# Two drains of GpSimd, behind the last gather and behind the third-last scatter

## The chip, the cores and the metric

The kernel runs on one core of a Trainium2 chip. The metric is the device time of one execution in microseconds (us), the lower the better. The engines are named as in the profile: PE is TensorE's matmuls and PEld its weight loads, DVE is VectorE, ACT is ScalarE, POOL is GpSimd, and SP is SyncE, which here only issues transfers. A "q" behind an engine's name (POOLq) marks an instruction that the engine's sequencer runs itself, such as a wait on a semaphore, a branch or a drain. A **drain** is one of these: an instruction with no operands, which each engine has at the program's start and end.

## What is computed

Linear attention without a softmax for 8 batches of 8 heads, a normalisation of each head's output, and then a mixture of experts on the resulting 4608 rows of 512: each row goes to the one expert of 8 that its logits favour.

```python
def _attn_ref(q, k, v, g_norm):
    kv = np.einsum('bhsd,bhse->bhde', k, v)
    out = np.einsum('bhsd,bhde->bhse', q, kv)
    rms = np.sqrt(np.mean(out * out, axis=-1, keepdims=True) + 1e-06)
    return (out / rms * g_norm).astype(np.float32)

def _moe_ref(x, w_gate, w_output_gate, w1, w2):       # x: 4608 x 512, 8 experts, hidden 1024
    logits = x @ w_gate
    e_idx = np.argmax(logits, axis=1)
    ...
    for e in range(E):
        mask = e_idx == e
        h = np.maximum(x[mask] @ w1[e], 0.0)
        ye = h @ w2[e]
        out[mask] = gate_w[mask, None] * eom[mask, e, None] * ye
```

## The kernel before, in words

The attention is computed tile by tile, and its rows are written to a tensor `xs` in device memory. A routing part finds, for every expert, which rows are its own, and leaves tables of row numbers: `gidx` to gather by, `oidx` to scatter by.

The experts' part is a list of 16 **runs**. Each expert runs twice: the first eight runs take 256 rows of each expert in order, as soon as the first part of the rows is routed; the other eight take the rest of each expert's capacity, from the fullest expert to the emptiest. `run(i, unit)` is one of them:

- `mm1(i, f)` for f from 0 to 7 is the first matrix product with its Relu (lines 287 to 297).
- `mm2(i, k, ...)` for each tile of up to 128 rows is the second product (lines 318 and 324). Its end is a copy out of PSUM by ScalarE (line 335; for a tile of at most 64 rows lines 331 to 333, with VectorE) and a **scatter** of the tile's rows to the output, issued by GpSimd (line 336).
- In the first product of run i, at f = 2, `gather(i + 1)` has GpSimd fetch the rows of the next run by indirect transfers (line 236), and at f = 3 `scale_rows(i + 1)` has GpSimd multiply them by the heads' norms (line 244). `stage(i + 1, k)`, in the second product, has VectorE copy one column (line 258) and TensorE transpose the tile (line 262).

The last run, number 15, has three tiles, of 128, 128 and 44 rows. As it is the last one, its second product takes them in the order 0, 2, 1, so that the tile of 44 rows is not at the end:

```python
        order = list(range(T))
        if last_run and half(i):
            order.insert(1, order.pop())
        for k in order:
            mm2(i, k, at.get(k, {}))
```

For the runs from number 7 on, the order of instructions on TensorE, ScalarE and VectorE is as the code is written, while GpSimd's and SyncE's is made by a scheduler, which puts an instruction at the place where it becomes ready. Each engine runs its own instructions in that order and waits on semaphores for the others. Every transfer that GpSimd issues has a semaphore that tells of its landing.

Behind the last run stands a loop (line 1086) for experts that have more rows than their capacity. It runs `nreg` times, which is read from memory at run time (line 1085) and is zero for these inputs, so all engines jump past its body. On the path that skips it, semaphores are raised as the body would have raised them. Then, at line 1154, the program ends: all engines drain and meet at a barrier, GpSimd clears the semaphores, and they meet again. GpSimd is the one that collects the others there.

Of the kernel before, what the change touches and what calls it, by code (L numbers as in the profile page):

```python
# [54 lines left out]
RUNS = [(e, 0, ROWS_A) for e in range(E)] + [(p, TA, CAP[p] - ROWS_A) for p in range(E)]  # L55
# [60 lines left out]
def tiles_of(i):  # L116

    _, t0, n = RUNS[i]
    return [(t0 + k, k * P, min(P, n - k * P)) for k in range(-(-n // P))]
# [6 lines left out]
def body(ctx: ExitStack, tc: tile.TileContext, kvm, rem, qT, wg, gn, w1, w2, kc, xs, tab, out):  # L126
    nc = tc.nc
# [36 lines left out]
    def take(shape, dt, name, free=free):  # L164

        i = free.pop(0)
        t = mem.tile(shape, dt, name=name, tag=f"slot{i}")
        held[id(t)] = (i, t)
        return t
# [16 lines left out]
    def wload(i, which, c):  # L186
        p = RUNS[i][0]
        r = take([P, 1024], F32, "wraw")
        w = w1 if which == 1 else w2
        src = w[p:p + 1, c] if i < E else w[ds(expert(p, nc.sync), 1), c]  # L190
        d = nc.sync.dma_start(out=r, in_=src.rearrange("o p x -> p (o x)"))
        raw[(i, which, c)] = r
        return d
# [31 lines left out]
    def drop(which, c):  # L225
        for w in wgt.pop((which, c)):
            give(w)
# [3 lines left out]
    def gather(i):  # L231
        p = RUNS[i][0]
        rows = xs[0:1 + EARLY * P] if i < E else xs
        for t, c0, M in tiles_of(i):
            x = take([P, XW], F32, "xg")
            nc.gpsimd.indirect_dma_start(  # L236
                out=x[:M, :], out_offset=None, in_=rows,
                in_offset=bass.IndirectOffsetOnAxis(ap=gidx[i // E][:M, p, t:t + 1], axis=0))
            xg[(i, t)] = x

    def scale_heads(x, eng):
        v = x[:, 0:DM].rearrange("p (h d) -> p h d", d=D)
        f = x[:, C_RMS:C_RMS + H].unsqueeze(2).to_broadcast([x.shape[0], H, D])
        eng.tensor_tensor(out=v, in0=v, in1=f, op=ALU.mult)  # L244

    def scale_rows(i):
        for t, c0, M in tiles_of(i):
            scale_heads(xg[(i, t)][:M], nc.gpsimd)
# [20 lines left out]
    def half(i):  # L269

        n = RUNS[i][2] % P
        return n if n <= P // 2 else 0

    def mm1(i, f):

        C = RUNS[i][2]
        T = half(i)
        hi, lo = ([a[:, d] for d in range(4)] for a in xT[i])
        wh, wl = wgt[(1, f // 2)]
        if f == 0:  # L280
            w = i // E
            hT[i] = rp_[w].tile([P, 8, 2 * (ROWS_A, CMAX)[w]], F32R, name="hT", tag="hT")
        ps = ps_h.tile([P, 512], F32, name="hps", tag="h")
        for d in range(4):
            o = d * 256 + (f % 2) * P
            for w, x, k in ((wh, hi, 0), (wh, lo, 1), (wl, hi, 2)):
                nc.tensor.matmul(ps[:, :C], w[:, o:o + P], x[d][:, :C],  # L287
                                 start=(d == 0 and k == 0), stop=(d == 3 and k == 2))
        h = hT[i][:, f]
        C0 = C - T  # L290
        if T % (P // 2) and f == 0:

            for c in (C0, C0 + P // 2):
                nc.vector.memset(hT[i].bitcast(F32)[:, :, c + T:c + P // 2], 0.0)
        nc.scalar.activation(h[:, 0:C], ps[:, :C], AF.Relu)  # L295
        for a, b, l in [(0, C0, C0 + P if T else C)] + ([(C0, C, C0 + P // 2)] if T else []):
            nc.vector.scalar_tensor_tensor(out=h[:, l:l + b - a], in0=ps[:, a:b], scalar=0.0,  # L297
                                           in1=h[:, a:b].bitcast(F32), op0=ALU.max, op1=ALU.subtract)
# [3 lines left out]
    def mm2(i, k, events):  # L302
        nonlocal ny
        t, c0, M = tiles_of(i)[k]
        C = RUNS[i][2]
        T = half(i)
        ps = ps_y[0].tile([P, DM], F32, name="yps", tag=f"y{ny % 2}")
        tl = tails.pop((i, t))
        for f in range(8):
            h = hT[i][:, f]  # L310
            wh, wl = wgt[(2, f // 2)]
            w0 = (f % 2) * DM
            w = [a[:, w0:w0 + DM] for a in (wh, wl)]
            if M == T:

                for b in (1, 0) if f == 0 else (0, 1):
                    rows = (1 + b) * P // 2
                    nc.tensor.matmul(ps[:rows], h[:, c0:c0 + rows], w[1 - b],  # L318
                                     start=(f == 0 and b == 1), stop=(f == 7 and b == 1))
            else:  # L320
                l0 = C - T + P if T else C
                hh, hl = h[:, c0:c0 + M], h[:, l0 + c0:l0 + c0 + M]
                for n, (a, b) in enumerate(((hh, w[0]), (hh, w[1]), (hl, w[0]))):
                    nc.tensor.matmul(ps[:M], a, b, start=(f == 0 and n == 0), stop=(f == 7 and n == 2))  # L324
            for e in events.get(f, ()):
                e()
        y = mem.tile([P, DM], F32, name="y", tag=f"y{ny % 3}")
        ny += 1
        if M == T:
            y2 = mem.tile([P, DM], F32, name="y2", tag="yb")  # L330
            nc.scalar.copy(y2[:M], ps[P // 2:P // 2 + M])
            nc.vector.tensor_tensor(out=y[:M], in0=ps[:M], in1=y2[:M], op=ALU.add)
            nc.vector.tensor_scalar(out=y[:M], in0=y[:M], scalar1=tl[:M, 0:1], scalar2=None, op0=ALU.mult)
        else:
            nc.scalar.activation(y[:M], ps[:M], AF.Copy, scale=tl[:M, 0:1])  # L335
        i_ = nc.gpsimd.indirect_dma_start(  # L336
            out=out, out_offset=bass.IndirectOffsetOnAxis(ap=oidx[i // E][:M, RUNS[i][0], t:t + 1], axis=0),
            in_=y[:M], in_offset=None, bounds_check=NTOK - 1, oob_is_err=False)
        tc.declare_no_dep(i_.ins, group="out", reason=nodep)
        tc.add_to_no_dep_group("out", i_.ins)  # L340


    rp_ = [main.enter_context(tc.tile_pool(name="ra", bufs=1)), None]
# [444 lines left out]
    def early():  # L788
# [38 lines left out]
        while routing:  # L827
            advance()
            if routing:
                constants(1)  # L830
                if n < PIECES:
                    next(rest)
                    n += 1
        gather(0)
        mark = c1.tile([P, 1], F32, name="mark")
        behind = nc.gpsimd.memset(mark, 0.0)
# [170 lines left out]
    def run(i, unit):  # L1007

        last_run = i + 1 == len(RUNS)
        for f in range(8):  # L1010
            mm1(i, f)
            if i == 0 and f in (0, 2):
                split(0, 1, f // 2 + 2)
            if f % 2:
                split(i, 2, f // 2)
                drop(1, f // 2)
                if not last_run:
                    wload(i + 1, 1, f // 2)
            if f == 2 and not last_run:
                gather(i + 1)  # L1020
            if f == 3 and not last_run:
                scale_rows(i + 1)
            unit(f)
        T = len(tiles_of(i))
        Tn = 0 if last_run else len(tiles_of(i + 1))
        at = {}

        def put(k, f, e, *a):
            at.setdefault(k, {}).setdefault(f, []).append(lambda: e(*a))

        if not last_run:
            for c in range(4):
                at_ = (c, 0) if T >= 4 else divmod(c * T * 2, 8)
                put(*at_, split, i + 1, 1, c)
                put(*at_, wload, i + 1, 2, c)
        places = [(k, f) for k in range(T) for f in (2, 5)]
        places = places[-Tn:] if Tn > len(places) - 2 else places[:-1]
        for x in range(Tn):
            put(*places[x * len(places) // Tn], stage, i + 1, x)
        if i < E:  # L1040

            for k in range(T):
                put(k, 3, unit, 8 + k)
                for f in (1, 3, 6, 7):
                    put(k, f, step)
        order = list(range(T))
        if last_run and half(i):
            order.insert(1, order.pop())
        for k in order:
            mm2(i, k, at.get(k, {}))  # L1050
        for c in range(4):
            drop(2, c)

# [22 lines left out]
    with tc.manual_schedule(engines={ET.PE, ET.Activation, ET.DVE}):  # L1076
        for i in range(E - 1, len(RUNS)):
            run(i, lambda n: next(listing, None))
# [105 lines left out]
```

## Time and profile before

| | |
|---|---|
| runs shown | 609.4, 610.83, 612.5 us (median 610.83) |
| the profiled execution | 609.33 us, of which the span is 607.5 |
| TensorE matmuls busy | 557.1 us, 92% of the span |
| VectorE, ScalarE, GpSimd busy | 341.1, 286.3 and 148.7 us |
| granted TensorE clock, mean over the span | 0.976 of full speed |
| transfers issued by GpSimd | 42 gathers, 42 scatters, 1 direct |

The span runs from the first to the last instruction of the program; 1.8 us of the execution lie around it. Busy time does not count register, branch, semaphore and drain instructions, so an engine that drains counts as idle. All times in the rows further down count from the span's start.

### The profile page before, as it was taken

How to read it: one execution, taken by the hardware profiler on the slowest of the kernel's cores; microseconds unless marked ns; L12 is line 12 of the kernel's file. 1: busy time of each engine (PE TensorE's matmuls, PEld its weight loads, DVE VectorE, ACT ScalarE, POOL GpSimd, SP SyncE). 2: the span in 40 equal slices, each digit the busy share in tenths (PEclk: the TensorE clock that was granted, in tenths of full speed). 3: DMA queues.
4: the chain of work that ended last, by engine and by line, in shares of the span. 5: the costliest groups of instructions: out<-in, count | busy, mean ns of one | idle time of the engine just before them, and what ended most of it. 6: DMA issues, size and time to landing. Idle time of an engine off the chain costs nothing.

```text
span 607.5 us, 12239 instructions
## 1 busy us (share of the span) xinstructions
PE 557.1 (92%) x4857; PEld 483.9 (80%) x4857; DVE 341.1 (56%) x676; ACT 286.3 (47%) x481; POOL 148.7 (24%) x139
## 2 busy tenths in 40 slices
PE   7777759999999978999899999999999999999991
PEld 5656649898888767989788879889897979888980
DVE  2127756746478988566595635446355554656530
ACT  1455316658486544556454434434454453444420
POOL 2000330030302140413616024042423415050110
PEclk9989879999999999999999999999999999999996
DMA  8998967988776655776827336363554636464100
GB/s 312 406 404 327 343 208 237 374 268 319 258 253 216 196 215 180 230 232 192 280 92 250 125 118 210 103 210 118 188 175 141 204 122 203 162 205 144 37 19 18
DMA packets 43163, 125.97 MB, mean 207 GB/s; under 512 B 10302, under 2 KB 10430, under 8 KB 43104
## 3 DMA queue, kind: packets, MB, share of 16 engines
q1 hardware_dynamic: 35920, 105.19, 50.6%
q0 software_dynamic: 6752, 19.75, 9.8%
q8 instruction: 40, 0.66, 0.4%
q10 hardware_dynamic: 432, 0.22, 0.1%
q14 instruction: 19, 0.16, 0.1%
HBM read 105.94 MB, written 19.75 MB: 207 GB/s over the span
## 4 chain that ended last, share of the span: by engine, by line
PE 70%; issue 10%; DVE 8%; DMA 5%; ACT 2%; POOL 2%; ACTq 0%; POOLq 0%; SPq 0%; DVEq 0%
PE yps L324 29%; PE hps L287 27%; PE ops L511 4%; PE kvps L436 3%; PE tps L262 3%; DMA ld<-qT 2%; DVE wlo L221 2%; DMA xg<-xs,gidx 2%; PE yps L318 1%; POOL out L336 1%; DMA wgs<-wg 1%; ACT whi L218 1%; PE cps L415 1%; DVE hT L297 1%; DVE la L690 1%
## 5 line engine op out<-in xcount | busy, mean ns | idle before, releaser
L287 PE MATMUL hps<-xT,whi 128*128 128x256 f32 (+8 forms) x1024 | 221.5, 309 | 9.6 <-DVE hT L297 8.2
L324 PE MATMUL yps<-whi,hT 128*128 128x512 f32 (+3 forms) x592 | 199.4, 400 | 0.0
L287 PEld LDWEIGHTS hps<-xT,whi 128*128 128x128 f32 x1024 | 169.7, 190 | 17.1 <-DVE hT L297 10.5
L287 PE MATMUL hps<-xT,wlo 128*128 128x256 f32 (+8 forms) x512 | 155.8, 304 | 0.0
L324 PEld LDWEIGHTS yps<-whi,hT 128*128 128x128 f32 (+3 forms) x592 | 110.1, 186 | 24.1
L336 POOL DMA_INDIRECT out<-y,oidx x42 | 45.8, 1090 | 317.6 <-ACT y L335 278.6
L297 DVE SCALAR_TENSOR_TENSOR hT<-hps,hT 128x256 fp32r<-128x256 f32 (+9 forms) x168 | 63.0, 394 | 97.2 <-ACT hT L295 97.0
L324 PE MATMUL yps<-wlo,hT 128*128 128x512 f32 (+3 forms) x296 | 115.9, 392 | 0.0
L295 ACT ACTIVATE hT<-hps 128x256 fp32r<-128x256 f32 (+8 forms) x128 | 54.8, 428 | 121.4 <-PE hps L287 120.6
L214 DVE SCALAR_TENSOR_TENSOR wlo<-wraw,gcol,whi 128x1024 fp32r<-128x1024 f32 x64 | 82.4, 1293 | 44.0 <-ACT whi L211 44.0
L287 PEld LDWEIGHTS hps<-xT,wlo 128*128 128x128 f32 x512 | 97.6, 191 | 0.3
L221 DVE TENSOR_TENSOR wlo<-wraw,whi 128x1024 fp32r<-128x1024 f32 x64 | 82.9, 1296 | 25.4 <-ACT whi L218 23.2
L211 ACT ACTIVATE whi<-wraw,gcol 128x1024 fp32r<-128x1024 f32 x64 | 72.9, 1149 | 0.0
L218 ACT CAST whi<-wraw 128x1024 fp32r<-128x1024 f32 x64 | 66.6, 1041 | 0.0
L324 PEld LDWEIGHTS yps<-wlo,hT 128*128 128x128 f32 (+3 forms) x296 | 55.2, 187 | 10.4
L244 POOL TENSOR_TENSOR xg<-xg 128x512 f32<-128x512 f32 (+8 forms) x40 | 48.1, 1206 | 45.7 <-DMA xg<-xs,gidx 45.3
L335 ACT ACTIVATE y<-yps,tl 128x512 f32<-128x512 f32 (+3 forms) x37 | 25.4, 686 | 64.1 <-PE yps L324 52.3
L236 POOL DMA_INDIRECT xg<-xs,gidx x42 | 46.6, 1110 | 16.3 <-issue 9.9
L265 ACT CAST xT<-tps 128x512 fp32r<-128x512 f32 (+8 forms) x42 | 23.0, 548 | 54.8 <-PE tps L262 53.9
L511 PE MATMUL ops<-aug,ld 64*64 64x80 f32 x1152 | 29.7, 239 | 11.3 <-DMA ld<-qT 5.3
L266 DVE TENSOR_TENSOR xT<-tps,xT 128x512 fp32r<-128x512 f32 (+8 forms) x42 | 26.7, 636 | 19.3 <-ACT xT L265 19.2
L511 PEld LDWEIGHTS ops<-aug,ld 64*64 64x64 f32 x1152 | 23.9, 136 | 17.1 <-issue 11.9
(148 smaller groups left out, 403.6 us busy)
## 6 DMA issues: line engine op xcount, KB each, us to landing
wraw<-w SPq DMA_DIRECT2D x128, 512.0 KB, 4.4
ld<-kvm SPq DMA_DIRECT2D x32, 512.0 KB, 8.5
ld<-qT SPq DMA_DIRECT2D x18, 512.0 KB, 8.1
xs<-xrow SPq DMA_DIRECT2D x18, 512.0 KB, 4.6
ld<-rem SPq DMA_DIRECT2D x4, 512.0 KB, 8.0
xg<-xs,gidx POOLq DMA_INDIRECT x42, 5.4
out<-y,oidx POOLq DMA_INDIRECT x42, 4.0
xs<-xtail SPq DMA_DIRECT2D x3, 80.0 KB, 3.7
```

Source lines behind the costliest of these rows:

```text
L211: he.activation(hi, r, AF.Copy, scale=gcol[:, 0:1])
L214: eng.scalar_tensor_tensor(out=lo, in0=r, scalar=gcol[:, 0:1], in1=hi.bitcast(F32), op0=ALU.mult, op1=ALU.subtract)
L218: he.copy(hi, r)
L221: eng.tensor_tensor(out=lo, in0=r, in1=hi.bitcast(F32), op=ALU.subtract)
L236: nc.gpsimd.indirect_dma_start(out=x[:M, :], out_offset=None, in_=rows, in_offset=bass.IndirectOffsetOnAxis(ap=gidx[i // E][:M, p, t:t + 1 ...
L244: eng.tensor_tensor(out=v, in0=v, in1=f, op=ALU.mult)
L287: nc.tensor.matmul(ps[:, :C], w[:, o:o + P], x[d][:, :C], start=(d == 0 and k == 0), stop=(d == 3 and k == 2))
L295: nc.scalar.activation(h[:, 0:C], ps[:, :C], AF.Relu)
L297: nc.vector.scalar_tensor_tensor(out=h[:, l:l + b - a], in0=ps[:, a:b], scalar=0.0, in1=h[:, a:b].bitcast(F32), op0=ALU.max, op1=ALU.subtract)
L324: nc.tensor.matmul(ps[:M], a, b, start=(f == 0 and n == 0), stop=(f == 7 and n == 2))
L336: i_ = nc.gpsimd.indirect_dma_start(out=out, out_offset=bass.IndirectOffsetOnAxis(ap=oidx[i // E][:M, RUNS[i][0], t:t + 1], axis=0), in_=y ...
L511: nc.tensor.matmul(ps[c0:c0 + D, u, p * W:(p + 1) * W], qt[g // 2][r, p, q0:q0 + D], augs[b % 3][r, p, :], start=True, stop=True)
```

## The change

`gather` now returns its last transfer, and `mm2` returns its scatter. A new function, `settle`, puts a drain into GpSimd's program, with a dependency that makes it wait for the landing of the transfer that it is given. It is called in two places: behind the gather for the last run (in run 14), and behind the scatter of the third-last tile of the last run. As that run has three tiles, this is its first scatter.

```diff
@@ gather, and a new function behind it
-            nc.gpsimd.indirect_dma_start(
+            gathered = nc.gpsimd.indirect_dma_start(
                 out=x[:M, :], out_offset=None, in_=rows,
                 in_offset=bass.IndirectOffsetOnAxis(ap=gidx[i // E][:M, p, t:t + 1], axis=0))
             xg[(i, t)] = x
+        return gathered
+
+    def settle(g_):
+
+        d_ = nc.gpsimd.drain()
+        tc.add_manual_dep(d_.ins, g_.ins.name,
+                          mybir.DependencyInfo(mybir.DependencyClass.Sync, mybir.DependencyReason.DATA),
+                          reason="order of GpSimd")
@@ mm2
         tc.add_to_no_dep_group("out", i_.ins)
+        return i_
@@ run, first product
             if f == 2 and not last_run:
-                gather(i + 1)
+                g_ = gather(i + 1)
+                if i + 2 == len(RUNS):
+                    settle(g_)
@@ run, second product
         for k in order:
-            mm2(i, k, at.get(k, {}))
+            g_ = mm2(i, k, at.get(k, {}))
+            if last_run and k == order[-3]:
+                settle(g_)
```

GpSimd's program from the last gather (three transfers) to the loop, before the change. `xg` are the gathered rows, `y` a tile's result; the semaphores DMASW0 to DMASW7 tell of GpSimd's own transfers, the others of engines:

```order
L236 DMA xg<-xs,gidx_75 44x528 [waits DMAHW4_49,Pool_49]
L244 TENSOR_TENSOR xg<-xg 128x512 [waits DMASW3_49]
L244 TENSOR_TENSOR xg<-xg 128x512 [waits DMASW4_49]
L336 DMA out<-y,oidx_77 4608x512 [waits DVE_49]
L244 TENSOR_TENSOR xg<-xg 44x512 [waits DMASW5_49]
L336 DMA out<-y,oidx_77 4608x512 [waits Activation_49]
L336 DMA out<-y,oidx_77 4608x512 [waits DMASW0_49,Activation_49]
L336 DMA out<-y,oidx_77 4608x512 [waits DMASW1_49,DVE_49]
L336 DMA out<-y,oidx_77 4608x512 [waits DMASW2_49,Activation_49]
L336 DMA out<-y,oidx_77 4608x512 [waits DVE_49]
L336 DMA out<-y,oidx_77 4608x512 [waits Activation_49]
L1085 TENSOR_LOAD novi [waits DVE_49]
```

The same place with the change. Drains have no row of their own here; the semaphore that a drain waits for is listed with the instruction behind it:

```order
L236 DMA xg<-xs,gidx_75 44x528 [waits DMAHW4_49,Pool_49]
L252 TENSOR_TENSOR xg<-xg 128x512 [waits DMASW3_49]
L252 TENSOR_TENSOR xg<-xg 128x512 [waits DMASW4_49]
L344 DMA out<-y,oidx_77 4608x512 [waits DVE_49]
L252 TENSOR_TENSOR xg<-xg 44x512 [waits DMASW5_49]
L344 DMA out<-y,oidx_77 4608x512 [waits Activation_49]
L344 DMA out<-y,oidx_77 4608x512 [waits DMASW0_49,Activation_49]
L344 DMA out<-y,oidx_77 4608x512 [waits DMASW1_49,DVE_49]
L344 DMA out<-y,oidx_77 4608x512 [waits DMASW2_49,Activation_49]
L344 DMA out<-y,oidx_77 4608x512 [waits DMASW2_49,DVE_49]
L344 DMA out<-y,oidx_77 4608x512 [waits Activation_49]
L1098 TENSOR_LOAD novi [waits DVE_49]
```

No instruction has moved on any engine (line 244 has become 252, 336 has become 344, 1085 has become 1098 and 1154 has become 1167). The first drain stands directly ahead of the scaling of the 44-row tile, behind the two scalings of 128 rows and the last scatter of run 13; it waits for the gather of those 44 rows, as the scaling itself did. The second stands between the last run's first and second scatter (the third-last and second-last of the rows above) and waits for the first one's landing, which nothing waited for at this place before.

## Rows read from the trace of the kernel before

**Rows 1.** The page: span, and busy time of each engine (share, instructions).

```profile
span 607.5 us, 12239 instructions
PE 557.1 (92%) x4857; PEld 483.9 (80%) x4857; DVE 341.1 (56%) x676; ACT 286.3 (47%) x481; POOL 148.7 (24%) x139
```

**Rows 2.** Stretches of the end: busy time by engine, granted clock, DMA share, GB/s.

```profile
core 0: us, PE busy (x) PEld busy (x) DVE busy (x) ACT busy (x) POOL busy (x), PEclk, DMA share, GB/s
...
587.00:596.00 9.00, 7.38 (x33) 5.58 (x31) 1.16 (x2) 1.27 (x2) 1.84 (x3) 1.00 0.08 31
596.00:599.00 3.00, 0.00 (x0) 0.00 (x0) 0.00 (x0) 0.00 (x0) 0.38 (x1) 0.90 0.21 81
599.00:606.00 7.00, 0.00 (x0) 0.00 (x0) 0.00 (x0) 0.00 (x0) 0.00 (x0) 0.50 0.01 2
```

**Rows 3.** DMA from 596 to 599.3: packets by queue; us from issue to landing.

```profile
q0 software_dynamic: 80, 0.24, 18.9%
...
out<-y,oidx POOLq DMA_INDIRECT x1, 2.7
```

**Rows 4.** Line 1154: ns min/median/max, first and last start in us.

```profile
L1154 POOLq EVENT_SEMAPHORE  x4: 17/17/17, 606.4 to 607.4; - x4
L1154 SPq DRAIN  x3: 7/7/13, 599.0 to 606.6; - x3
L1154 POOLq DRAIN  x3: 46/98/7017, 599.3 to 606.9; - x3
L1154 ACTq DRAIN  x2: 8/8/8, 599.2 to 606.6; - x2
L1154 DVEq DRAIN  x2: 10/14/17, 599.4 to 606.7; - x2
L1154 PEldq DRAIN  x2: 8/40/72, 599.8 to 606.7; - x2
...
L1154 PEldq EVENT_SEMAPHORE  x2: 51/51/51, 606.6 to 607.5; - x2
```

**Rows 5.** GpSimd's timeline: start and duration in us, instruction, idle time before it.

```profile
536.00 0.97 POOL L236 DMA_INDIRECT xg<-xs,gidx  x1 [0.30 <-issue]
537.28 0.93 POOL L236 DMA_INDIRECT xg<-xs,gidx  x1 [0.31 <-issue]
...
543.72 1.05 POOL L244 TENSOR_TENSOR xg<-xg 44x512 f32<-44x512 f32 x1
557.73 1.37 POOL L336 DMA_INDIRECT out<-y,oidx  x1 [12.96 <-ACT y L335]
...
586.30 0.99 POOL L336 DMA_INDIRECT out<-y,oidx  x1 [16.49 <-ACT y L335]
591.08 0.95 POOL L336 DMA_INDIRECT out<-y,oidx  x1 [3.79 <-DVE y L333]
595.39 0.99 POOL L336 DMA_INDIRECT out<-y,oidx  x1 [3.37 <-ACTq L1086]
```

**Rows 6.** Line 1086, GpSimd alone: columns as in rows 4.

```profile
L1086 POOLq EVENT_SEMAPHORE  x14: 17/43/43, 595.9 to 599.1; - x14
L1086 POOLq COMPARE_BRANCH  x3: 33/38/48, 595.8 to 599.2; - x3
L1086 POOLq INC_SWDGE_SEM  x1: 1895/1895/1895, 596.0 to 596.0; - x1
```

**Rows 7.** DMA from 599 to 606.3: busy tenths in 40 slices, packets by queue.

```profile
DMA  0000000000300000000000000000000000000000
...
DMA packets 1, 0.02 MB, mean 2 GB/s; under 512 B 0, under 2 KB 0, under 8 KB 0
...
q8 instruction: 1, 0.02, 0.8%
```

**Rows 8.** Line 1138, the program's start: columns as in rows 4.

```profile
L1138 POOLq INC_SWDGE_SEM  x1: 27/27/27, 0.1 to 0.1; - x1
...
L1138 POOLq DRAIN  x1: 167/167/167, 0.3 to 0.3; - x1
```

**Rows 9.** The page's DMA queues (packets, MB, share) and issues, whole span.

```profile
q0 software_dynamic: 6752, 19.75, 9.8%
q8 instruction: 40, 0.66, 0.4%
...
xg<-xs,gidx POOLq DMA_INDIRECT x42, 5.4
out<-y,oidx POOLq DMA_INDIRECT x42, 4.0
...
xs<-xtail POOLq DMA_DIRECT2D x1, 2.1 KB, 6.4
```

**Rows 10.** Who reads the gathered rows from 559 to 562: columns as in rows 4.

```profile
L262 PE MATMUL tps<-ident,xg x4: 232/233/255, 560.6 to 560.8; 44*128 44x44 f32 x4
L258 DVE COPY tl<-xg x1: 139/139/139, 559.7 to 559.7; 44x1 f32<-44x1 f32 x1
```

**Rows 11.** All scatters of line 336: us from issue to landing.

```profile
DMA to landing us min/median/max: 2.0/4.0/7.2
```

## The prediction

> **What bounds the kernel now.** I read the page first, then the stretches behind 587 us, then line by line what stands in the last 12 us, then GpSimd's own timeline from the last gathers on. The page says that TensorE is busy for 92% of 607.5 us and GpSimd for 24% [rows 1]; the change touches GpSimd alone, so the question is where GpSimd is waited for. In the stretches the reader is to see that the work ends long before the span does: TensorE's matmuls end in the stretch 587 to 596, and from 599 to 606 no engine is busy at all and DMA moves at 2 GB/s [rows 2]; in between, the last scatter's 80 packets move [rows 3]. What stands in these 7 us is a drain of GpSimd at line 1154: it starts at 599.3 and takes 7017 ns; the drains of the other four engines that meet it there took 7 to 72 ns, and the last of those, TensorE's, started at 599.8 [rows 4]. GpSimd collects the others behind its drain, so all of them stand still until it has its next event semaphore at 606.4 [rows 4].
>
> What is this drain waiting for? Not for a transfer: the last scatter is issued at 595.4 [rows 5] and lands 2.7 us later [rows 3], so at 598.1, 1.2 us before the drain starts, and GpSimd's waits for the DMA semaphores are over at 599.1 [rows 6]. Between 599 and 606.3 the queues carry one packet, a code load of 0.02 MB [rows 7]. Not for another engine either: a wait shows as a gap ahead of an instruction, not as its duration (TensorE's event semaphore behind the barrier has 51 ns, though it waited from 599.9 to 606.6 [rows 4]). And a drain by itself is cheap on this engine: the two that follow took 98 and 46 ns, the one at the program's start, behind four short memsets, 167 ns [rows 4, 8]. What lies between the cheap one at the start and the dear one at the end is 42 gathers, 42 scatters and one direct DMA issued by GpSimd, 6752 packets on its queue [rows 9]. So the reading that I take is that each of these DMAs leaves GpSimd something to finish, that it does not do this while it is idle, and that a drain makes it do so.
>
> **The change, part by part.** Nothing is removed and nothing else moves: the two drains are the only new instructions on any engine, each with one wait.
>
> The price of a drain. If the 7017 ns are shared by the 85 DMAs, with the middle one of the cheap drains, 98 ns, as what a drain costs anyway, one DMA leaves (7017 - 98) / 85 = 81 ns. No row shows a second drain behind DMAs, so this is bounded from both sides: 0 ns for each DMA, with the whole 7.0 us as a fixed price that any drain pays behind any DMA; and 81 ns with no fixed price. I take 81, because the only row with nothing behind it is at 0.1 us and the only row with 85 DMAs behind it is at 7.0.
>
> The Trainium skill speaks against this change in "VectorE: DVE Perf Modes", section "The DRAIN you can't avoid": drains around a program are there a constant boilerplate of about 12 ns on all five engines. Here four engines agree (7 to 72 ns), and GpSimd does not (46 to 7017). By that rule the two drains cost 24 ns, take nothing from the end, and the time stays 610.5 us.
>
> Drain one stands ahead of the 44-row scaling of line 244 (L244), behind the last of three gathers. Its own wait costs nothing, since the scaling waited for the same gather. Before it are all 42 gathers, the direct DMA and 36 scatters (6 of the 42 come later), 79 DMAs: 79 x 81 + 98 = 6.5 us. In the profile the scaling starts at 543.7 and takes 1.05 us; it would start at 550.2 and end at 551.3 [rows 5]. What hides this is idle time of GpSimd: its next instruction, a scatter, starts at 557.7 [rows 5], and the rows scaled here are first wanted at 559.7 by VectorE's copy and at 560.6 by TensorE's four 44-row transposes [rows 10]. So 6.5 us lie in 12 us of room (543.7 to 557.7, less the scaling and the scatter's waits). If the cover were gone, each microsecond past 11.9 would delay a scatter, which nobody waits for; past 15, VectorE's copy and then the transposes.
>
> Drain two stands between the first and the second scatter of the last run and waits for the first's landing: issued at 586.3, landing 2.7 us later by the row of the last scatter [rows 3, 5], thus about 589.0. Behind it stands the scatter of 591.1. With 4 DMAs since drain one it takes 4 x 81 + 98 = 0.4 us and ends at 589.4, 1.7 us ahead of that scatter: nothing is late. The third scatter starts at 595.4, and two DMAs of GpSimd have started 1.28 us apart [rows 5], so the second could start as late as 594.1 before the third, and with it the end, is late. Were the first scatter to need the 7.2 us of the slowest one [rows 11], drain two would end at 593.9, still in time.
>
> The last drain then has 2 DMAs behind it: 2 x 81 + 98 = 0.26 us, from 599.3 to 599.6. What is late next is TensorE's drain, which starts at 599.8 and takes 72 ns [rows 4]; the barrier passes at about 599.9 in place of 606.4. The gain is 606.4 - 599.9 = 6.5 us, and the 1.1 us from 606.4 to the span's end stay.
>
> **The sum.** The profiled execution took 609.33 us with a span of 607.5; it becomes 609.3 - 6.5 = 602.8. It is the lowest of the four known executions (609.4, 610.83, 612.5 and this one), whose mean is 610.5; from that mean the forecast is 610.5 - 6.5 = 604.0 us, 1.1% less. What a measurement can tell from no change is about 0.5%, 3 us.
>
> **The rivals.** *A fixed price (ends slower).* If any drain behind any DMA takes 7.0 us, say because it visits every queue however little it holds, drain one is hidden all the same (550.7), the last one still takes 7.0, and drain two runs from 589.0 to 596.0. The second scatter goes to 596.1 and the third to 597.4, 2.0 us late: 610.5 + 2.0 = 612.5 us. The mixed case decides between this and mine: with a fixed part f the end gains about 6.9 - f, and loses what f exceeds 5 us (589.1 to 594.1) in drain two; the signs meet near f = 6. At f = 2 the gain is 4.7 us (605.8), at f = 4 it is 2.7 (607.8). For a fixed part speaks that there is one dear row only; against it that 98 and 46 ns follow directly on the dear one, so the visit would have to know that nothing had come since.
>
> *Nothing changes.* The 7 us belong to the end of the program (the code load at 601.0 falls into them, or the semaphore increment of line 1086, L1086, on the path that skips the loop, which took 1895 ns here and 27 at the start [rows 6, 8]), or to what the last DMA alone leaves behind. Then the new drains take 0.1 us each and the time is 610.5. Against it: the code load is one packet, over long before 606; and the increment at the start had a drain of 167 ns behind it. The Trainium skill, "PSUM — Partial Sum Buffer", section "Engine vs sequencer instructions", says that a drain waits until its engine is fully idle. The trace agrees as far as it goes: GpSimd has no instruction left at 599.3, so what keeps it busy is inside it.
>
> *Another engine takes the place.* The packet of 599 to 606 is a load of TensorE's code by its queue, q8, whose 40 loads of 0.66 MB in all [rows 9] fit the engine with by far the most instructions. If TensorE needs it for its next instruction, behind the barrier, it must come first: it moves in the eleventh of 40 slices from 599 to 606.3, so at about 601.0, 1.2 us behind the start of TensorE's drain, and takes 0.9 us (0.8% of 16 engines over 7.3 us [rows 7]), so the end waits until about 602 in place of 600 and the gain is 4.5 us: 606.0 us. For it speaks only that the load is there; against it that the next instruction stands right behind that drain in TensorE's program, and the drain ran with no load ahead of it since 599.
>
> **How the numbers follow.** My forecast has 0.62. TensorE's code has 0.07. A part of the price fixed, between 2 and 6 us, has 0.11, and half of it or a little more gives over 3 us. A price fixed altogether has 0.11; nothing changes, 0.09. The rule of the Trainium skill on boilerplate drains ("VectorE: DVE Perf Modes") belongs to this last case. Faster by over 0.5% is thus 0.62 + 0.07 + 0.06 = 0.75. Slower by over 0.5% needs over 3 us, a fixed price of more than 8 in drain two, which no row has: 0.02. The rest, 0.23, is within 0.5%.
>
> The likeliest case by itself lies between 602.0 (the lowest known execution less the whole drain of 7.0, and 0.3 below) and 606.0 (6.5 from the highest of the runs, 612.5). The range must take in TensorE's code and the mixed cases, which end at about 609, and a part of the cases without change around 610.5; what remains outside is the upper part of those, under 2 in 10. The range is 601.8 to 610.2.
>
> **What would show it.** In the changed kernel's profile a drain at 543 to 544 of about 6.5 us shows the shared price right; one of 0.1 us shows that the backlog is not there. Drain two near 589 tells the fixed part directly: 0.4 us is mine, 7.0 the rival's. The last drain should be 0.2 to 0.4 us, with TensorE's drain as the last to arrive. The scatters of the last run must keep their places at 586, 591 and 595, and the transposes at 560 must not wait for the scaling. My prediction is wrong if the last drain keeps several microseconds although the first two took their share, or if something else holds the barrier between 600 and 606.

## The result, and the profile after

The changed kernel takes 604.0 us (median of 4 runs, 602.51 to 604.67), the kernel before 610.74 us (4 runs). The ratio is 0.9885 with a 95% interval of 0.9853 to 0.9916: 1.1% faster, 6.7 us, and the whole interval lies beyond 0.5%. The prediction was 604.0.

The profiled execution took 602.51 us with a span of 600.7. The page's first lines, and the stretches of the end (busy time by engine, clock, DMA share, GB/s), which answer to [rows 1] and [rows 2]:

```profile
span 600.7 us, 12241 instructions
...
PE 559.4 (93%) x4857; PEld 486.3 (81%) x4857; DVE 339.3 (56%) x676; ACT 286.2 (48%) x481; POOL 149.2 (25%) x139
```

```profile
587.00:596.00 9.00, 6.98 (x31) 5.32 (x29) 1.16 (x2) 1.27 (x2) 1.93 (x2) 1.00 0.08 31
596.00:599.00 3.00, 0.00 (x0) 0.00 (x0) 0.00 (x0) 0.00 (x0) 0.00 (x0) 0.92 0.21 81
599.00:601.00 2.00, 0.00 (x0) 0.00 (x0) 0.00 (x0) 0.00 (x0) 0.00 (x0) 0.50 0.03 8
```

Two instructions more, the same counts of work on every engine, and the stretch without work behind 599 us is 1.7 us long in place of 8.5. The drains and waits at the program's end (now line 1167; ns min/median/max, first and last start in us) answer to [rows 4]:

```profile
L1167 POOLq EVENT_SEMAPHORE  x4: 17/17/17, 599.6 to 600.6; - x4
...
L1167 POOLq DRAIN  x3: 46/98/204, 598.9 to 600.4; - x3
...
L1167 DVEq DRAIN  x2: 10/14/17, 599.0 to 599.9; - x2
L1167 PEldq DRAIN  x2: 8/40/72, 599.5 to 599.9; - x2
...
L1167 PEldq EVENT_SEMAPHORE  x2: 51/51/51, 599.8 to 600.7; - x2
```

GpSimd's drain takes 204 ns where it took 7017. It ends at 599.1, and TensorE's, which starts at 599.5, is now the last to arrive: the barrier passes at 599.6. The two new drains (the helper's line 244; one window around each):

```profile
L244 POOLq DRAIN  x1: 8677/8677/8677, 541.8 to 541.8; - x1
...
L244 POOLq DRAIN  x1: 376/376/376, 588.6 to 588.6; - x1
```

And GpSimd's timeline around them (start and duration in us, instruction, idle time before it), which answers to [rows 5]:

```profile
541.28 1.55 POOL L252 TENSOR_TENSOR xg<-xg 128x512 f32<-128x512 f32 x1 [0.43 <-DMA xg<-xs,gidx]
543.00 0.98 POOL L344 DMA_INDIRECT out<-y,oidx  x1 [0.17 <-issue]
550.61 1.04 POOL L252 TENSOR_TENSOR xg<-xg 44x512 f32<-44x512 f32 x1 [6.63 <-issue]
557.25 1.37 POOL L344 DMA_INDIRECT out<-y,oidx  x1 [5.61 <-ACT y L343]
...
585.90 0.99 POOL L344 DMA_INDIRECT out<-y,oidx  x1 [16.56 <-ACT y L343]
590.67 0.95 POOL L344 DMA_INDIRECT out<-y,oidx  x1 [3.79 <-DVE y L341]
594.99 0.99 POOL L344 DMA_INDIRECT out<-y,oidx  x1 [3.37 <-ACTq L1099]
```

The first drain's 8677 ns begin while GpSimd still has a scaling and a scatter ahead of it. From the scatter's end (543.00 + 0.98 = 543.98) to the drain's (541.8 + 8.7 = 550.5) are 6.5 us. That scatter is still in flight when the drain gets to work; it lands 2.9 us behind 543.0, inside the drain (DMA from 543 to 551):

```profile
out<-y,oidx POOLq DMA_INDIRECT x1, 2.9
```

The 44-row scaling stands 6.9 us later than before and still ends at 551.7, ahead of its readers:

```profile
L270 PE MATMUL tps<-ident,xg x4: 232/233/255, 560.1 to 560.4; 44*128 44x44 f32 x4
L266 DVE COPY tl<-xg x1: 139/139/139, 559.3 to 559.3; 44x1 f32<-44x1 f32 x1
```

From the issue of the last scatter to the barrier there were 606.4 - 595.4 = 11.0 us, and there are 599.6 - 595.0 = 4.6: the tail is 6.4 us shorter. The last scatter also stands 0.4 us earlier in this execution, which no step of the change explains; in e1 below, whose program is the same up to the second drain, it stands at 595.7.

### The profile page after: what moved, and what is told of

The parts are those of the page before. It is cut to its first block, busy times and chain, and to the rows that moved or that the text cites. A ratio compares the mean times of both kernels' runs of the same rounds, so it can differ in the third digit from the quotient of the medians.

```text
span 600.7 us, 12241 instructions
## 1 busy us (share of the span) xinstructions
PE 559.4 (93%) x4857; PEld 486.3 (81%) x4857; DVE 339.3 (56%) x676; ACT 286.2 (48%) x481; POOL 149.2 (25%) x139
## 3 DMA queue, kind: packets, MB, share of 16 engines
q0 software_dynamic: 6752, 19.75, 10.0%
## 4 chain that ended last, share of the span: by engine, by line
PE 80%; DVE 7%; DMA 5%; issue 4%; ACT 3%; POOL 0%; POOLq 0%; ACTq 0%; SPq 0%; DVEq 0%
PE hps L295 32%; PE yps L332 32%; PE ops L520 4%; PE kvps L445 3%; PE tps L270 3%; DMA ld<-qT 2%; PE yps L326 2%; DVE wlo L221 2%; ACT whi L218 1%; DMA wgs<-wg 1%; PE cps L424 1%; DMA xg<-xs,gidx 1%; DVE hT L305 1%; DVE wlo L214 1%; ACT xrow L525 0%
## 5 line engine op out<-in xcount | busy, mean ns | idle before, releaser
L295 PEld LDWEIGHTS hps<-xT,whi 128*128 128x128 f32 x1024 | 169.8, 190 | 16.0 <-DVE hT L305 10.2
L214 DVE SCALAR_TENSOR_TENSOR wlo<-wraw,gcol,whi 128x1024 fp32r<-128x1024 f32 x64 | 81.9, 1285 | 44.0 <-ACT whi L211 44.0
```

The costliest lines, as they stand in the source:

```text
L214: eng.scalar_tensor_tensor(out=lo, in0=r, scalar=gcol[:, 0:1], in1=hi.bitcast(F32), op0=ALU.mult, op1=ALU.subtract)
L295: nc.tensor.matmul(ps[:, :C], w[:, o:o + P], x[d][:, :C], start=(d == 0 and k == 0), stop=(d == 3 and k == 2))
```

## The experiments

My theory was that each DMA that GpSimd issues leaves it 82 ns of work that only a drain does, (7017 - 204) / (85 - 2), with about 40 ns for the drain itself. The rivals: a price paid once, by the first drain behind DMAs; a price by the time since the last drain; a price by the rows or packets that were moved. The changed kernel's three drains (79, 4 and 2 DMAs) do not tell the theory from the first two with certainty, since the counts, the times and the order run together there.

**e1, the first drain alone.** The changed kernel without

```diff
-            if last_run and k == order[-3]:
-                settle(g_)
```

> The first drain alone (behind the last gather); the second is left out. Price shared by the DMAs, 82 ns for each since the last drain and about 0.04 us: 6 scatters stand between it and the end, so the last drain takes 6 x 82 + 40 = 0.53 us, ends at 599.4, and TensorE's drain (ends 599.6 in the changed kernel) still comes later: 604.0 us, the same as with both. Price by time since the last drain (7.0 us in 599, 12 ns per us): 48 us give 0.6 us, the same time. Price paid once, by the first drain behind DMAs: the last drain takes 0.2 us or less, 604.0.

604.08 us (6 runs), ratio to the kernel before 0.9901 (0.9873 to 0.9929): no difference to the changed kernel that this can tell. Its end:

```profile
L1165 POOLq EVENT_SEMAPHORE  x4: 17/17/17, 600.2 to 601.3; - x4
...
L1165 POOLq DRAIN  x3: 98/194/542, 599.6 to 601.0; - x3
...
L1165 PEldq DRAIN  x2: 7/39/71, 600.1 to 600.5; - x2
```

With 6 DMAs behind it the last drain takes 542 ns and ends together with TensorE's. The second drain of the change is worth nothing that these runs show. A price paid once falls: it would leave about 200 ns here.

**e2, the second drain alone.**

```diff
                 g_ = gather(i + 1)
-                if i + 2 == len(RUNS):
-                    settle(g_)
```

> The second drain alone (behind the first scatter of the last run). Price shared: it has 83 DMAs behind it, 83 x 82 + 40 = 6.85 us, from 588.6 to 595.5; the second scatter goes from 590.7 to 595.6, the third 1.3 us behind it to 596.9 in place of 595.0, so the end is 1.9 us later than with both drains; the last drain 0.2 us: 605.9 us. Paid once or by time: the drain takes about 7, the same collision. A price that can be worked off only when the engine has been idle for long would show less than 6.8.

605.81 us (9 runs), ratio 0.9932 (0.9904 to 0.9961). The drain, and GpSimd's timeline behind it:

```profile
L244 POOLq DRAIN  x1: 6851/6851/6851, 589.2 to 589.2; - x1
```

```profile
586.44 0.99 POOL L344 DMA_INDIRECT out<-y,oidx  x1 [16.60 <-ACT y L343]
596.93 0.95 POOL L344 DMA_INDIRECT out<-y,oidx  x1 [9.50 <-issue]
598.19 0.99 POOL L344 DMA_INDIRECT out<-y,oidx  x1 [0.30 <-POOLq L1097]
```

The drain with 83 DMAs behind it runs into the scatter that waits behind it, as the rival of the prediction said it would with a price of 7 us at this place. The first scatter stands 0.5 us later than in the changed kernel and the third 3.2 us later, so 2.7 us are the collision's in this execution (1.9 expected: 0.9 us pass from the drain's end at 596.0 to the second scatter); by the medians of e1 and e2 it costs 1.7 us.

**e3, one drain in the middle.**

```diff
-                if i + 2 == len(RUNS):
+                if i + 1 == E:
                     settle(g_)
...
-            if last_run and k == order[-3]:
-                settle(g_)
```

> One drain alone, moved forward: behind the gather for run 8, in run 7, with 35 DMAs ahead of it and 50 behind. Price shared: 35 x 82 + 40 = 2.9 us there (beside work that GpSimd still has in flight), and the last drain takes 50 x 82 + 40 = 4.1 us in place of 0.2: the barrier passes about 3.4 us later than in the changed kernel, 607.4 us. Paid once: the last drain takes 0.2 us, 604.0 us. By time: the drain stands at about 300 us, so 3.6 us there and 3.6 at the end, 606.9.

607.03 us (12 runs), ratio 0.9944 (0.9921 to 0.9967). The two drains:

```profile
L244 POOLq DRAIN  x1: 5589/5589/5589, 301.7 to 301.7; - x1
...
L1165 POOLq DRAIN  x3: 98/194/4135, 599.5 to 604.5; - x3
```

The last drain takes 4135 ns for 50 DMAs, where a price paid once leaves 200. Time is harder to tell apart here (3.6 expected). The drain in the middle missed: a scatter ahead of it ends its issue at 303.3, the drain ends at 307.3, so it took 4.0 us where 35 DMAs are worth 2.9. e7 looks into that.

**e4, more DMAs and no drain.** The kernel before with a scratch tensor `scr` and, behind each scatter,

```diff
+        nc.gpsimd.dma_start(out=scr[ny:ny + 1, :].rearrange("o (a x) -> (o a) x", x=16), in_=cf[0:33, 0:16])
```

> The kernel before, with 42 more direct DMAs of GpSimd, each 33 rows of 64 B of a constant to a scratch tensor that nothing reads; most are issued early. No drain is added. Price shared by DMAs whatever they move: the last drain takes 127 x 82 + 40 = 10.4 us in place of 7.0. Shared by rows (9790 rows in 7.0 us, 0.7 ns each): 42 x 33 rows add 1.0, 8.0 us. By time, or by indirect DMAs alone: 7.0 us.

One execution, 619.32 us. The last drain, the semaphore increment ahead of it, and GpSimd's DMA queue over the span:

```profile
L1156 POOLq DRAIN  x3: 46/98/10447, 606.2 to 617.2; - x3
```

```profile
L1087 POOLq INC_SWDGE_SEM  x1: 2746/2746/2746, 602.0 to 602.0; - x1
```

```profile
q0 software_dynamic: 8096, 19.85, 9.6%
```

The drain takes 10447 ns: 42 DMAs more cost 3430, or 82 each. Each of them is 2 KB in 32 packets ((8096 - 6752) / 42), against 79 packets of an average DMA before. So it is the DMA that is paid for, not its rows, packets or bytes, and a direct one costs what a gather or scatter does. The time since the last drain, 606 us, is 1% longer than before [rows 4] and the drain 49%: price by time falls too. The rest of what this kernel loses lies ahead of the drain: its last scatter is issued at 601.1 in place of 595.4, and that was not looked into.

**e5, both drains without their wait.** The dependency orders the drain behind the transfer, but has it wait for nothing:

```diff
-                          mybir.DependencyInfo(mybir.DependencyClass.Sync, mybir.DependencyReason.DATA),
+                          mybir.DependencyInfo(mybir.DependencyClass.NoSync, mybir.DependencyReason.SCHED_ONLY),
```

> Both drains without their wait for a landing, kept in place by order alone: the first stands behind three gathers in flight (78 DMAs ahead of it), the second directly behind the first scatter of the last run, which is in flight (5 more). If a drain works off what was issued, landed or not: 78 x 82 + 40 = 6.4 us and 5 x 82 + 40 = 0.45 us behind the end of the DMA ahead, last drain 0.2 us, 604.0 us. If it works off only what has landed: the second shows 0.4 or less and the last one more than 0.2 (3 DMAs, 0.29). If a drain waits for the landing by itself: the second takes about 2 us, until 588.6, and the time is 604.0 all the same.

602.7 us (4 runs), ratio 0.9854 (0.983 to 0.9877); its interval overlaps that of the change. The two drains, the last gather and the scatter behind which they stand, and the median time to landing of the three gathers and that of the scatter:

```profile
L244 POOLq DRAIN  x1: 10196/10196/10196, 536.7 to 536.7; - x1
...
L244 POOLq DRAIN  x1: 3217/3217/3217, 587.5 to 587.5; - x1
```

```profile
539.53 0.93 POOL L236 DMA_INDIRECT xg<-xs,gidx  x1 [0.31 <-issue]
...
587.73 0.99 POOL L344 DMA_INDIRECT out<-y,oidx  x1 [16.57 <-ACT y L343]
```

```profile
xg<-xs,gidx POOLq DMA_INDIRECT x3, 5.2
...
out<-y,oidx POOLq DMA_INDIRECT x1, 2.7
```

The scatter is issued until 588.7 and lands at 590.4; the drain ends at 587.5 + 3.2 = 590.7, 0.3 us behind the landing, and not at 588.7 + 0.45. So a drain waits for the transfers in flight, with no semaphore asked. The explicit wait of the change is not needed for this, and the second drain's duration here holds a wait. The first one ends at 536.7 + 10.2 = 546.9, 6.4 us behind the end of the last gather's issue (540.5). That is what 78 DMAs are worth, though three gathers were in flight when their issue ended.

**e6, a drain behind every gather.**

```diff
                 g_ = gather(i + 1)
-                if i + 2 == len(RUNS):
-                    settle(g_)
+                settle(g_)
...
-            if last_run and k == order[-3]:
-                settle(g_)
```

> A drain behind every gather of runs 1 to 15 (15 drains, 4 to 7 DMAs apart), none in the last run. Price shared: each takes 0.04 + 82 ns per DMA since the one before, 0.37 to 0.61 us plus what GpSimd still has in flight, together 79 x 0.082 + 15 x 0.04 = 7.1 us; the last drain has 6 DMAs, 0.54 us: 604.0 us if the waits for the gathers hold nothing up, as the scalings behind them wait for the same. Where a scatter stood between a gather and its scaling, the drain's wait delays it, and a run that is short of time could lose 1 to 3 us: up to 607.

603.84 us (6 runs), ratio 0.9869 (0.9846 to 0.9892): again the same as the change. The first seven drains (one window), and the last of the program:

```profile
L244 POOLq DRAIN  x7: 364/364/481, 92.3 to 282.8; - x7
```

```profile
L1164 POOLq DRAIN  x3: 46/98/537, 603.4 to 604.4; - x3
```

Six drains with 4 DMAs each take 364 ns and one with 5 takes 481. Of the eight later ones all but one take 2.5 us and more; in each of them a transfer of GpSimd lands within the drain. Fifteen drains lose nothing that the runs show.

**e7, the middle drain with nothing in flight.** As e3, but behind the scaling, with a wait for the last scatter ahead (`sent` collects the scatters):

```diff
             if f == 3 and not last_run:
                 scale_rows(i + 1)
+                if i + 1 == E:
+                    settle(sent[-1])
```

> The middle drain again, but behind the last scaling of run 8's rows and with a wait for the scatter ahead of it, so that none of the 35 DMAs is in flight. The drain of e3 took 4.0 us from the end of that scatter's issue, 1.1 over the 2.9 expected. If the excess is the scatter's landing, this drain takes 35 x 82 + 40 = 2.91 us; if the price is not the same for each DMA, 4.0. The last drain stays at 50 DMAs, 4.14 us, in either case.

One execution, 606.15 us. The two drains:

```profile
L244 POOLq DRAIN  x1: 2931/2931/2931, 308.0 to 308.0; - x1
...
L1168 POOLq DRAIN  x3: 98/193/4129, 598.9 to 603.9; - x3
```

2931 ns for 35 DMAs, and 4129 for 50 as in e3. With nothing in flight the excess of e3 is gone. A transfer in flight does not always cost that, though: the first drain of the changed kernel has a scatter in flight as well, e5's has three gathers, and both end 6.5 and 6.4 us behind the last issue, which is the price of their 79 and 78 DMAs alone.

## Why the prediction was right

**The price.** With nothing in flight, all kernels together:

| DMAs since the drain before | drain, ns | kernel |
|---|---|---|
| 2 | 204 | the change |
| 4 | 376 (364) | the change (e6) |
| 5 | 481 | e6 |
| 6 | 542 (537) | e1 (e6) |
| 35 | 2931 | e7 |
| 50 | 4135 (4129) | e3 (e7) |
| 83 | 6851 | e2 |
| 85 | 7017 | before |
| 127 | 10447 | e4 |

(10447 - 204) / 125 = 81.9 ns for each DMA, and 204 - 2 x 81.9 = 40 ns for the drain. The prediction had 81 and 98, from one dear row and the cheap ones. There is no fixed part of microseconds, so the mixed cases go with the fixed price.

**The three drains.** Forecast 6.5, 0.4 and 0.26 us; measured 6.5 (behind the scatter), 0.38 and 0.20. The covers held: 5.6 us of idle time are left between the first drain's scaling and the next scatter, and the second drain ends at 589.0, 1.7 us ahead of its scatter. That the first drain waits for the scatter in flight too was not in the forecast; that landing fell inside the 6.5 us and cost nothing, which was luck, as e3 shows a scatter in flight that cost 1.1 us.

**What comes next.** TensorE's drain, as forecast, at 599.5 + 0.07; the barrier at 599.6 (forecast 599.9, for a last scatter that stood 0.4 us later). The tail gained 6.4 us, the forecast said 6.5. That the median meets 604.0 to the tenth is luck too: the four runs lie 2.2 us apart.

**Two slips in the working.** The room for the first drain was 557.73 - 543.72 - 1.05 = 13.0 us by [rows 5], less some tenths for the scatter's waits, and not 11.9. And by its own formula, 6.9 - f, the mixed case gains 4.9 us at f = 2 and 2.9 at f = 4, not 4.7 and 2.7. The forecast rests on neither.

**The rivals.** "Nothing changes" falls with the 204 ns. The fixed price falls with 376 and 204, though its collision is real: e2 shows it where one drain has to do all the work. TensorE's code was no obstacle. The one load of q8 from 599.5 to 602 moves in the twelfth of 40 slices, so from 600.2, behind the barrier that all engines pass at 599.8:

```profile
q8 instruction: 1, 0.02, 2.7%
```

Its 1.1 us (2.7% of 16 engines over 2.5 us) reach past the span's end at 600.7, so no instruction waited for it.

The Trainium skill's rule of boilerplate drains ("VectorE: DVE Perf Modes", "The DRAIN you can't avoid") speaks of about 12 ns from the runtime's preamble and postamble. Taken for the drains at the program's end, which have a line of the kernel, it fits four engines (7 to 72 ns) and not GpSimd, whose drains go from 46 to 10447 ns by what it has issued. The Trainium skill's rule that a drain waits until the engine is fully idle ("PSUM — Partial Sum Buffer", "Engine vs sequencer instructions") agrees with e5, where idle includes transfers in flight.

**A premise that was wrong.** I argued that a wait shows as a gap and not as a duration. That does not hold on GpSimd, nor on TensorE's queue, by the waits behind the loop (line 1099 of the changed kernel), which answer to [rows 6]:

```profile
L1099 POOLq EVENT_SEMAPHORE  x14: 17/43/1612, 595.5 to 598.6; - x14
...
L1099 POOLq INC_SWDGE_SEM  x1: 233/233/233, 595.6 to 595.6; - x1
...
L1099 PEldq EVENT_SEMAPHORE  x12: 51/51/1862, 595.8 to 599.1; - x12
```

One event semaphore of GpSimd has 1612 ns and one of TensorE 1862, in which the last scatter lands, and e5's second drain holds a landing. The conclusion stood on the other leg: at 599.3 that scatter had landed for 1.2 us.

**Which part does it.** The first drain alone gives the whole gain (e1); the second is worth nothing beside it that the runs show, and by itself it gives less of the gain (e2).

## What to carry to other kernels

Look at the program's last microseconds by line: a drain that takes microseconds while nothing moves is work that can be done earlier. Where GpSimd issues many DMAs, count them, multiply by the measured 82 ns, and put one drain into a stretch where GpSimd is idle for that long and its next instruction is not urgent; the few DMAs behind it cost little at the end. Watch what waits behind the drain and what is in flight ahead of it, since the drain waits for that as well (e5).

## What the runs showed that I had not expected

The semaphore increment on the path that skips the loop pays for the same DMAs: it takes 233 ns with 2 since the last drain (the change), 319 with 6 (e1), 1199 with 50 (e3), 1895 with 85 [rows 6] and 2746 with 127 (e4), so (2746 - 233) / 125 = 20 ns each, on top of 193. It does not work them off: the drain behind it still pays for all. In the kernel before its 1895 ns lay beside the landing of the last scatter, which is why the 1.7 us that it became shorter are not in the gain.

In e3, with 35 DMAs and one transfer in flight, the drain took 1.1 us more than the 2.9 of the quiet one (e7); in the change and in e5, with 79 and 78 DMAs and one and three transfers in flight, it took nothing more. In what order the drain goes through them, and why the wait and the work add up in part in e3 and not in the other two, no run here shows.
